# A Fourier filter plus a gated MLP: the first four token tiles transposed in fp32, with another order of instructions

## The chip, the cores and the metric

The kernel runs on one core of a Trainium2 chip. TensorE (PE) multiplies matrices into PSUM; VectorE (DVE) and ScalarE (ACT) work elementwise and read PSUM; GpSimd (POOL) does small work in SBUF; SyncE (SP) issues the DMAs. The metric is the device time of one execution in microseconds (us), the median of several runs.

## The reference

The input x has 2048 tokens of 448 features. The output is a sum of three terms: x itself, a Fourier filter and a gated MLP, the last two on the layer-normalised x.

```python
xn = layernorm(x)                                       # over the 448 features
filter = irfft2(rfft2(xn) * (w_r + 1j * w_i))           # over tokens and features
h = relu(xn @ W_gate) * (xn @ W_up)                     # 448 -> 1792
return x + filter + h @ W_down                          # 1792 -> 448
```

## The kernel before, in words

**Splits.** Every large factor in fp32 is split into a high fp16 part and a low one (the rest), and products are made as high x high + low x high + high x low. So each weight slab costs ACT a scaling to the high half (`whi`, `w_hi`), and DVE a scale-and-subtract to the low half (`wlo`, `w_lo`). Before that ACT squares the slab (`wsq`), GpSimd sums over the partitions (`par`), and DVE makes a power of two from the sum (`wex`, `wsc`). A slab is one of two halves (`g0` gate, `g1` up) of one of 14 blocks (`W0` to `W13`) of the 1792 hidden features; it comes with one 256 KB DMA (`lw`).

**Tokens.** The 2048 tokens lie in 16 tiles `n2` of 128; tile `n2` belongs to chunk q = n2 % 4, and the chunks are worked on in the order 0, 2, 1, 3. A chunk's normalised tokens must stand transposed (features on partitions) as the moving operand: `Tq[q]`, nine rows of [128, 512] fp16. Rows 0 to 2 are the high halves of features 0 to 383, rows 5 to 7 their low halves, and rows 3, 4 and 8 hold the last 64 features, high and low, with a copy of every eighth feature in the other half of the partitions.

**How chunk 0 gets there before.** Its four tiles are loaded (`lx0`, `lx4`, `lx8`, `lx12`), their mean and variance taken on DVE (`bn`, `ag`), and the reciprocal deviation made in two groups A (tiles 0, 4) and B (8, 12) with a square root on ACT (`sq`) and small steps on DVE (`ra` to `rd`, `rm`). Then, for each tile: `xn` (DVE; for tile 4 `an4` on ACT) writes normalised fp32; `hi` (ACT, `ln_hi`) writes its fp16 high half into a tile `tt`; `lo` (DVE, `ln_lo`) the low half; `tpA` and `tpB` (PE, `ln_tp`) transpose three 128x128 fp16 blocks each; `evA` and `evB` (`ln_ev`, a prefix says whether on DVE or ACT) copy them from PSUM into `Tq`. For the last 64 features of all four tiles `tpC` (`ln_tpc`) makes 24 half-width transposes, and three copies (`evC0` to `evC2`, `ln_evc`) bring them to `Tq`. Chunk 2 and the later ones go through fp16 tiles and transposing DMAs (`dm`) instead; the change doesn't touch how they are made.

**Keeping PE busy.** While PE has nothing to do, `keep_warm` issues 512-wide products of a cleared tile into unused PSUM: 16 at the start (`warm`, after GpSimd has cleared that tile) and 4 more a little later (`kw4`).

**The first products.** For block W0 and chunk 0 they are cut up so that they can start early: `hh` (high x high), `lh` (low weight x high tokens), `hl` (high weight x low tokens), each for one of two slabs and one of two 256-column halves (tiles 0 and 4, then 8 and 12): `hh01` is slab 0, half 1. Each has three 256-wide products. `ml` adds the one of rows 3 and 4; then come `hp0` (four products with 64-row weights, shared with W1), and whole slabs `gu1g0`, `gu1g1` and so on. After a block's products ACT and DVE make relu(gate) x up and split it (`re`, `tm`, `gh`, `gl`).

**What sets the order.** The text `OPENING` lists the steps of the opening by these names, and every engine carries out its own in exactly that order (`fixed`). Behind it a planner, `Order.place`, places each instruction by keys and a model of costs (`cost`, `matmul`, `dma`), and its result is the order on each engine. The Fourier filter's work on DVE runs in the background of the MLP, and its matmuls are grouped as 34 "runs" of 64-row shapes (`order.run`), 8 each of four kinds and 2 small ones. A run that is ready interrupts the stream of MLP products only when it has waited longer than its `hold`, when PE is in a 64-row shape already, or when the stream would have to wait. Every instruction appears in the profile under the line of `place` that issues it, L416, so groups are told apart by tile name: `wst` is the loaded slab, `wt` the split weight, `y` fp32 buffers (the tokens of the opening among them), `arena` a region with many small tiles (the `tt` tiles, the identity, the warm tile), `gu`, `dn`, `fx` PSUM banks, `g` and `h` the MLP's results.

Of the kernel before, what the change touches and what calls it, by code (L numbers as in the profile page):

```python
# [34 lines left out]
lx0 lx4 bn0 lx12 bn4 lx8 lw ag0 lid lw ag4 sqA raA rbA rcA warm rdA rmA xn0 bn12 bn8 an4 ag12 hi0 ag8 lo0 hi4 sqB tpA0  # L35
wsqW0g0 lx14 lw tpB0 raB lo4 rbB rcB tpB4 kw4 rdB rmB aevA0 wsqW0g1 lw xn8 tpA4 parW0g0 wexW0g0 lx6 lw vevB4 hi8 vevB0
hi12 wscW0g0 vevA4 whiW0g0 lx10 tpA8 aevA8 tpA12 parW0g1 lo8 tpB8 wsqW1g1 hh00 hl00 wsqW1g0 lw lw lw xn12 vevA12 hh01
lo12 wexW0g1 wloW0g0 parW1 wscW0g1 tpB12 whiW0g1 vevB12 lx2 tpC aevC1 bn6 lwd3 lh01 lh00 wexW1 wscW1 vevB8 hh10 vevC0
whiW1g0 wloW0g1 hl10 wloW1g0 whiW1g1 wloW1g1 hl11 bn10 bn2 bn14 hh11 lwd0 wsqW3g1 ml0 ml1 wsqW2g0 wsqW2g1 lh11 wsqW3g0
parW2 lfd ag2 hl01 ag10 lh10 ag14 ag6 hp0 re0 tm0 lw lwd1 sqC raC wexW2 lw gu1g0 rbC wscW2 rcC rdC xn14 parW3 wexW3  # L40
whiW2g1 wloW2g1 lwd4 gu1g1 hi14 cp14 wscW3 xn2 whiW2g0 lo14 wloW2g0 whiW3g0 hi2 lwd2 whiW3g1 wsqW4g0 xn10 re1 wsqW4g1
parW4 wloW3g0 hi10 cp2 ly0 tm1 gu2g1 gu2g0 cp10 ly4 wdq0 wdq4 wloW3g1 wexW4 gh0 xn6 wdq3 lo10 hp2 gu3g0 hi6 re2 ly12
wscW4 whiW4g0 lo2 whiW4g1 gu3g1 lo6 wdq2 gh1 tm2 dm14 wdq1 gl0 wloW4g0 gu4g0 ly8 dm10 wloW4g1 gl1 cp6 gu4g1 re3 gh2
tm3 wdp wdsc gh3 gl3 aevC2 wdh1 dm2 gl2 wdl1 wdh4 dm6 wdh3 wdl4 hp4 re4 wdl3 tm4 wdh0 wdl0 wdh2 wdl2 gh4 gl4
# [376 lines left out]
def tile_gfnet_reglu(ctx: ExitStack, tc: tile.TileContext, x, xr, wgu, wd, wf, ident, c_fd, c_fm, c_im, c_row, c_id,  # L421
                     out):
    nc = tc.nc
    order = Order()
# [300 lines left out]
    def ln_tpc(q):

        b = (fx(), fx())
        for i in range(3):
            tp["end", i] = b[i // 2].bitcast(F16)[:, 512 * (i % 2):512 * (i % 2) + 512]
        for j in range(4):  # L730
            t = tt[q + 4 * j].rearrange("p a b -> p (a b)")
            c, l = t[:, 384:448], t[:, 1024:1088]
            for i, half in enumerate(((c, t[:, 7:512:8]), (l, c), (l, t[:, 647:1152:8]))):
# [1068 lines left out]
```

## Time and profile before

| | us |
|---|---|
| median of 3 runs | 434.8 (433.99 to 435.23) |
| the profiled execution | 434.42 |
| its span on the core | 432.6 |
| PE / DVE / ACT / POOL busy | 425.2 / 384.0 / 262.7 / 30.1 |
| DMA | 38.63 MB in 37721 packets |

How to read the rows below: a row of a timeline is start, length (both us), engine, line, operation, output <- input by tile name, shape, and count; in brackets the idle time of the engine before it and what ended it. A group's row ends in busy time, mean ns of one, and idle time before. A busy PE row includes the latency of its last product, so the spacing of products is read from several in a row. The length of a PE row is not PE at its peak speed.

### The profile page before, as it was taken

What the parts mean: (1) busy time and instruction counts of PE and PEld (TensorE: products, weight loads), DVE (VectorE), ACT (ScalarE), POOL (GpSimd) and SP (SyncE); (2) the same over time, 40 slices, a digit from 0 to 9 for tenths busy, and PEclk for the clock granted to TensorE, in tenths of its full rate; (3) what the DMA queues carried; (4) which work ended last, traced back from release to release, by engine and by line L of the source; (5) the groups of instructions that cost most, each with busy time, mean ns of one, the idle gap of its engine ahead of it and who ended that gap; (6) DMA issues with size and microseconds to landing.
All of it is one profiled execution on the core that took longest, in us unless ns stands there. A gap on an engine that the chain in (4) does not pass through costs nothing.

```text
span 432.6 us, 8471 instructions
## 1 busy us (share of the span) xinstructions
PE 425.2 (98%) x3222; PEld 202.8 (47%) x3222; DVE 384.0 (89%) x804; ACT 262.7 (61%) x495; POOL 30.1 (7%) x72
## 2 busy tenths in 40 slices
PE   7999999999999999999999999999999999999996
PEld 3644544444444445445444444444554554545554
DVE  6998989999988899999999999999999999993443
ACT  5898466387447938645534634763666765864661
POOL 1140013042001100000000110100000000000000
PEclk9999999999999999999999999999999999999999
DMA  8859319009104703343504300040222121310212
GB/s 258 300 120 258 137 44 233 16 7 218 58 3 131 232 14 113 89 123 84 153 18 104 99 1 0 2 95 8 51 53 45 49 75 24 94 44 2 85 45 86
DMA packets 37721, 38.63 MB, mean 89 GB/s; under 512 B 18928, under 2 KB 33072, under 8 KB 37680
## 3 DMA queue, kind: packets, MB, share of 16 engines
q1 hardware_dynamic: 37680, 38.09, 31.9%
q8 instruction: 25, 0.41, 0.4%
q14 instruction: 16, 0.13, 0.1%
HBM read 23.20 MB, written 3.67 MB: 62 GB/s over the span
## 4 chain that ended last, share of the span: by engine, by line
DVE 47%; PE 34%; ACT 6%; issue 5%; DMA 4%; SPq 3%; DVEq 0%; POOL 0%; ACTq 0%
PE gu L416 23%; DVE y L416 19%; DVE arena L416 13%; PE dn L416 8%; DVE g L416 5%; DVE h L416 4%; PE fx L416 3%; SPq L416 3%; DVE wst L416 2%; ACT arena L416 2%; DVE wt L416 2%; DMA arena<-in_wf 1%; ACT h L416 1%; DMA wst<-in_wgu 1%; ACT y L416 1%
## 5 line engine op out<-in xcount | busy, mean ns | idle before, releaser
L416 PE MATMUL gu<-T,wt 128*128 128x512 f16 (+2 forms) x1250 | 264.4, 376 | 0.0
L416 PEld LDWEIGHTS <-wt 128*128 128x128 f16 (+1 forms) x1250 | 111.4, 97 | 144.0 <-issue 21.6
L416 PE MATMUL dn<-wdt,h 128*128 128x448 f16 x648 | 125.8, 353 | 0.6 <-ACT dn L416 0.5
L416 PEld LDWEIGHTS <-h 128*128 128x128 f16 x684 | 66.0, 98 | 61.8 <-issue 2.6
L416 ACT ACTIVATE h<-g 128x512 f16<-128x512 f32 x56 | 35.1, 628 | 54.5 <-DVE g L416 54.3
L416 DVE TENSOR_TENSOR y<-y 128x464 f32<-128x464 f32 (+2 forms) x82 | 58.8, 745 | 2.3 <-ACT y L416 1.5
L416 DVE TENSOR_TENSOR arena<-arena 128x116 f32<-128x116 f32 (+6 forms) x105 | 52.9, 525 | 4.3 <-ACT arena L416 2.8
L416 ACT ACTIVATE g<-gu 128x512 f32<-128x512 f32 x56 | 32.8, 586 | 34.0 <-PE gu L416 33.9
L416 DVE SCALAR_TENSOR_TENSOR g<-gu,g 128x512 f32<-128x512 f32 x56 | 38.3, 684 | 16.5 <-ACT g L416 13.4
L416 DVE TENSOR_TENSOR h<-g,h 128x512 f16<-128x512 f32 x56 | 38.4, 688 | 4.5 <-ACT h L416 3.8
L416 ACT ACTIVATE xy<-dn,dsc 128x448 f32<-128x448 f32 x44 | 27.5, 625 | 21.0 <-PE dn L416 20.5
L416 DVE TENSOR_TENSOR wst<-wst 128x116 f32<-128x116 f32 (+2 forms) x96 | 30.7, 375 | 0.7
L416 DVE SCALAR_TENSOR_TENSOR y<-y 128x232 f32<-128x232 f32 (+2 forms) x52 | 30.0, 599 | 0.5
L416 ACT ACTIVATE dn<-xy,dinv 128x448 f32<-128x448 f32 x44 | 27.8, 636 | 1.4 <-DMA xy<-in_x 0.3
L416 PEld LDWEIGHTS <-arena 64*128 64x128 f16 (+2 forms) x836 | 17.3, 96 | 14.3 <-issue 6.2
L416 DVE SCALAR_TENSOR_TENSOR wt<-wst,wsc,wt 128x512 f16<-128x512 f32 x28 | 20.2, 745 | 2.3 <-ACT wt L416 2.2
L416 ACT ACTIVATE arena<-arena 128x116 f32<-128x116 f32 (+3 forms) x33 | 15.0, 465 | 10.7 <-DMA arena<-in_wf 7.5
L416 POOL PARTITION_ALL_REDUCE wm<-wm x15 | 8.8, 588 | 175.0 <-DVE y L416 94.3
L416 ACT ACTIVATE wt<-wst,wsc 128x512 f16<-128x512 f32 x28 | 19.0, 711 | 1.8 <-DVE wsc L416 1.8
L416 POOL COPY arena<-arena 128x56 f16<-128x56 f16 (+1 forms) x36 | 15.9, 474 | 59.7 <-ACT arena L416 53.8
L416 ACT ACTIVATE junk<-wst 128x512 bf16<-128x512 f32 x28 | 17.4, 622 | 1.9 <-DMA wst<-in_wgu 1.5
L416 PE MATMUL fx<-arena 64*128 64x64 f16 (+3 forms) x484 | 17.8, 245 | 0.7 <-DVE T L416 0.5
(81 smaller groups left out, 294.2 us busy)
## 6 DMA issues: line engine op xcount, KB each, us to landing
wst<-in_wgu SPq DMA_DIRECT2D x28, 256.0 KB, 4.7
arena<-in_wf SPq DMA_DIRECT2D x16, 232.0 KB, 3.2
arena<-y SPq DMA_DIRECT2D x64, 58.0 KB, 2.0
arena<-wst SPq DMA_DIRECT2D x32, 116.0 KB, 2.3
y<-in_xr SPq DMA_DIRECT2D x16, 224.0 KB, 4.5
xy<-in_x SPq DMA_DIRECT2D x16, 224.0 KB, 4.1
out<-xy SPq DMA_DIRECT2D x15, 224.0 KB, 2.0
wdst<-in_wd SPq DMA_DIRECT2D x14, 224.0 KB, 3.3
```

Of the source, the lines that this page charges most:

```text
L416: fn(*a, **k)
```

## The change

For chunk 0, `xn` now writes fp32 (all four on DVE) straight into the memory of the `tt` tiles, seen as fp32. `tp` transposes three 128x128 fp32 blocks of it against an fp32 identity. `ath` or `vth` (`ln_th`; the order names `ath`, ACT, four times) copies the three blocks from PSUM to fp16, which makes the high half; `tl` (DVE, `ln_tl`) subtracts that from PSUM, which makes the low half. For the last 64 features `tpC` makes 8 fp32 products with the identity. `aend0` (ACT) copies them out as high halves (row 3), `end1` moves half of that to row 4 with a DMA inside SBUF on SP's queue, `end2` (DVE) and `end3` (DVE, late) make the low halves. `hi`, `lo`, `tpA`, `tpB`, `evA`, `evB` and `evC` of chunk 0 are gone. Because the `tt` tiles hold fp32 first, GpSimd clears two regions in each at the start instead of one, and clears one more in each later (`z0` to `z3`).

The warming products become 10 at the start, and `kw1`, `kw1`, `kw5` around `tp0` and `tp4`. The planner gets one waiting time for each of the 34 runs instead of four times 3.0, one margin `SOON` for each engine (0.1 to 0.4) instead of 0.2 for all, a delay of 0.4 for ACT's steps that wait for DVE, and slightly other costs of DVE and of fp32 matmuls. `OPENING` is a new list.

```diff
-NWARM = 16
+NWARM = 10
-HOLDS = 3.0, 3.0, 3.0, 3.0
+HOLDS = (2, 3, 3, 3, 3, 3, 3, 3, 5, 3, 3, 2, 6, 3, 3, 8, 3, 2, 3, 3, 3, 6, 3, 0.5, 10, 5, 0.5, 3, 10, 3, 2, 3, 6, 3)
+SOON = dict(P=0.4, V=0.1, A=0.2, G=0.2, S=0.1)
+LATE = 0.4
+lx0 lx4 bn0 bn4 lx8 ag0 ag4 sqA raA rbA rcA rdA bn8 xn0 lx12 lw warm lid bn12 wsqW0g0 ag8 ag12 sqB kw1 tp0 xn4 rmA raB
+ath0 lw rbB kw1 tp4 rcB lw wsqW0g1 parW0g0 wexW0g0 wscW0g0 lw whiW0g0 rdB tl0 ath4 xn8 xn12 wsqW1g0 wloW0g0 kw5 tp8
+tp12 ath8 tpC parW0g1 wexW0g1 wsqW1g1 wscW0g1 hh00 tl4 tl8 ath12 tl12 parW1 lh00 aend0 wexW1 lx2 wscW1 whiW0g1 whiW1g0
+whiW1g1 wloW0g1 end2 lx6 wloW1g0 wloW1g1 hh01 lwd3 lw lh01 bn6 hl00 lw hl01 hh10 lw hh11 lw lh11 end1 lx14 hl11 lh10
+hl10 ml0 z0 lx10 bn10 ml1 wsqW3g1 bn2 lwd0 hp0 bn14 ag2 wsqW2g0 wsqW2g1 ag10 lwd2 ly4 z1 lw ag14 re0 ag6 wsqW3g0 lwd1
...
-    ISSUE = dict(V=-0.083, A=-0.098, G=-0.06)
-    SOON = 0.2
+    ISSUE = dict(V=-0.079, A=-0.098, G=-0.06)
...
-            return 0.15 + 1.04e-3 * n + 0.06 * ap
+            return 0.155 + 1.042e-3 * n + 0.06 * ap
...
-        return half, quads, 0.42 if x.dtype == F32 else op.n[0] / 2400 + 0.0025
+        return half, quads, (0.42 if rows <= 64 else op.n[0] / 1100) if x.dtype == F32 else op.n[0] / 2400 + 0.0025
...
-            far = 0.04 if op.node.eng == "S" or op.node.fixed else self.SLACK
+            far = dict(S=0.04 if e == "S" or op.node.fixed else self.SLACK)
+            if e == "A" and not op.node.fixed:
+                far["V"] = LATE
...
+    hold = iter(HOLDS).__next__
...
-    id_t = ft([128, 128], F16, "id_t")
+    id_t = ft([128, 128], F32, "id_t")
...
-    for t in tts:
-        G.memset(t[:, 3:9:5, 64:128], 0.0)
+    xts = [t.rearrange("p a b -> p (a b)").bitcast(F32) for t in tts]
+    for t, u in zip(tts, xts):
+        G.memset(u[:, 448:512], 0.0)
+        G.memset(t[:, 8, 64:128], 0.0)
...
+        if n2 % 4 == CHUNKS[0]:
+            xn[n2] = xts[n2 // 4][:, 0:D]
...
+    def ln_zero(i):
+        G.memset(tts[i][:, 3, 64:128], 0.0)
...
+    def ln_tp(n2):
+        j = n2 // 4
+        b = (side[1], *side[0], side[2])[j]
+        tp[n2] = b[:, 0:384].rearrange("p (a b) -> p a b", b=128)
         for a in range(3):
+            P.transpose(tp[n2][:, a, :], xn[n2][:, 128 * a:128 * a + 128], id_t)
...
+    def ln_th(n2, act):
+        js = slice(128 * (n2 // 4), 128 * (n2 // 4) + 128)
+        copy(Tq[n2 % 4][:, 0:3, js], tp[n2], act)
+
+    def ln_tl(n2):
+        T, js = Tq[n2 % 4], slice(128 * (n2 // 4), 128 * (n2 // 4) + 128)
+        V.tensor_tensor(T[:, 5:8, js], tp[n2], T[:, 0:3, js], op=OP.subtract)
...
+        tp["end"] = side[1]
+        for j, x in enumerate(xts):
+            js = slice(128 * j, 128 * j + 128)
+            for h, c in ((0, slice(384, 448)), (1, slice(7, 512, 8))):
+                P.matmul(tp["end"][64 * h:64 * h + 64, js], x[:, c], id_t, start=j == 0, stop=True,
+                         skip_group_check=True)
+
+    def ln_end(q, i, act=False):
+        T, a = Tq[q], tp["end"]
+        if i == 0:
+            copy(T[:, 3, :], a, act)
+        elif i == 1:
+            Q.dma_start(T[64:128, 4, :], T[0:64, 3, :])
+        elif i == 2:
+            V.tensor_tensor(T[0:64, 4, :], a[0:64], T[0:64, 3, :], op=OP.subtract)
+        else:
+            V.tensor_tensor(T[:, 8, :], a, T[:, 3, :], op=OP.subtract)
...
-        with order.run(HOLDS[0]):
+        with order.run(hold()):
```

More of the change, by code (lines that the diff above doesn't have):

```diff
@@ L34 @@
 OPENING = """
[L35 to L44, printed above, removed]
+lx0 lx4 bn0 bn4 lx8 ag0 ag4 sqA raA rbA rcA rdA bn8 xn0 lx12 lw warm lid bn12 wsqW0g0 ag8 ag12 sqB kw1 tp0 xn4 rmA raB
[3 more added lines that the diff above has]
+hl10 ml0 z0 lx10 bn10 ml1 wsqW3g1 bn2 lwd0 hp0 bn14 ag2 wsqW2g0 wsqW2g1 ag10 lwd2 ly4 z1 lw ag14 re0 ag6 wsqW3g0 lwd1
+tm0 sqC gu1g0 parW2 parW3 raC gu1g1 wexW2 re1 rbC wscW2 rcC lw rdC whiW2g1 z2 wexW3 xn14 wscW3 wloW2g1 whiW2g0 wsqW4g0
+whiW3g0 hi14 wsqW4g1 cp14 lwd4 wloW2g0 xn2 hi2 gu2g1 tm1 whiW3g1 lo14 xn10 ly12 cp2 parW4 wloW3g0 gu2g0 wloW3g1 wexW4
+gh0 hi10 hp2 cp10 ly8 z3 xn6 lo10 wdq0 wdq4 hi6 wscW4 ly0 whiW4g0 re2 gu3g1 lo2 gh1 lo6 wdq3 whiW4g1 gu3g0 wdq2
+wloW4g0 end3 tm2 gl0 dm14 wdq1 gl1 dm10 wloW4g1 re3 gu4g0 gh2 cp6 wdp dm2 lfd rmB gu4g1 tm3 dm6 wdsc gh3 gl3 wdh1 hp4
+gl2 wdl1 wdh4 re4 wdh3 wdl4 tm4 wdl3 wdh0 wdl0 wdh2 gh4 wdl2 gl4
 """
@@ L319, in lag @@
             pe = op.node.eng == "P"
-            far = 0.04 if op.node.eng == "S" or op.node.fixed else self.SLACK
-            return max([d.end + (far if d.node.eng == "S" else 0.04) for d in op.deps
-                        if not (pe and d.node.eng == "P")], default=0.0)
+            e = op.node.eng
+            far = dict(S=0.04 if e == "S" or op.node.fixed else self.SLACK)
+            if e == "A" and not op.node.fixed:
+                far["V"] = LATE
+            return max([d.end + far.get(d.node.eng, 0.04) for d in op.deps if not (pe and d.node.eng == "P")],
+                       default=0.0)
         def open_(n):
@@ L351, in pick @@
                 t = [est(n) for n in r]
-                lo = min(t) + self.SOON
+                lo = min(t) + SOON[e]
                 return min(((n, u) for n, u in zip(r, t) if u <= lo), key=lambda v: v[0].key)
@@ L357, in pick @@
                 return None
-            run = min(runs, key=lambda v: (v[1] > free["P"] + self.SOON, v[0].key)) if runs else None
+            run = min(runs, key=lambda v: (v[1] > free["P"] + SOON["P"], v[0].key)) if runs else None
             if head is None:
@@ L365, in pick @@
             now = max(free["P"], max(bank.values()))
-            if self.matmul(head.ops[0])[0][0] == 64 and h[1] <= now + self.SOON:
+            if self.matmul(head.ops[0])[0][0] == 64 and h[1] <= now + SOON["P"]:
                 return h
@@ L719, in copy @@
             V.tensor_copy(o, i)
-    def ln_ev(n2, part, act):
-        q, j = n2 % 4, n2 // 4
-        copy(Tq[q][:, 5 * part:5 * part + 3, 128 * j:128 * (j + 1)], tp[n2, part][:, 0:3], act)
-    def ln_tpc(q):
[L727 to L733, printed above, removed]
-                for h in range(2):
-                    P.transpose(tp["end", i][64 * h:64 * h + 64, 128 * j:128 * j + 128], half[h], id_t)
-    def ln_evc(q, i, act):
-        copy(Tq[q][:, (3, 4, 8)[i], :], tp["end", i], act)
+    def ln_th(n2, act):
[4 more added lines that the diff above has]
+        V.tensor_tensor(T[:, 5:8, js], tp[n2], T[:, 0:3, js], op=OP.subtract)
+    def ln_tpc(q):
+        tp["end"] = side[1]
[12 more added lines that the diff above has]
+            V.tensor_tensor(T[0:64, 4, :], a[0:64], T[0:64, 3, :], op=OP.subtract)
+        else:
+            V.tensor_tensor(T[:, 8, :], a, T[:, 3, :], op=OP.subtract)
     fi, sfx = {}, {}
@@ L826, in f_sdft @@
         sfx[a] = ps
-        with order.run(HOLDS[1]):
+        with order.run(hold()):
             for k in range(2):
@@ L1033, in row_dft @@
         y = state["rowps"] = fx()[:, 0:NG * KC]
-        with order.run(HOLDS[0]):
+        with order.run(hold()):
             for a in range(2):
@@ L1116, in i_sdft @@
         sps[p] = ps
-        with order.run(HOLDS[2]):
+        with order.run(hold()):
             for b in range(2):
@@ L1157, in i_ddft @@
             A.activation(sides[e], xy2[:, a, :, 224 * e:224 * (e + 1)], AF.Copy, scale=fsc[:, 2:3])
-        with order.run(HOLDS[3]):
+        with order.run(hold()):
             for k, n2 in enumerate((a, b)):
@@ L1681, in tile_gfnet_reglu @@
     G.memset(warm, 0.0)
-    wps = dn_bank(), dn_bank()
+    side[1], side[2] = dn_bank(), fx()
+    wps = dn_bank()
     side[0] = gu_bank()
```

47 lines of the change are left out of this document (15 added, 32 removed).

## The prediction

> **What bounds the kernel now.** I read the page's busy line first, then busy time by stretch, then TensorE's (PE's) own timeline of the opening, then the other engines' rows there, and last who waits for whom late in the kernel.
>
> The busy table by stretch gives: us, then busy time of PE, its weight loads (PEld), VectorE (DVE), ScalarE (ACT) and GpSimd (POOL), with counts.
>
> ```profile
> span 432.6 us, 8471 instructions
> PE 425.2 (98%) x3222; PEld 202.8 (47%) x3222; DVE 384.0 (89%) x804; ACT 262.7 (61%) x495; POOL 30.1 (7%) x72
> ...
> 0.00:15.10 15.10, 11.56 (x78) 6.06 (x79) 10.65 (x38) 10.09 (x21) 2.56 (x12) 1.00 0.88 295
> 15.10:43.00 27.90, 27.90 (x192) 13.54 (x192) 25.46 (x67) 25.30 (x56) 6.79 (x16) 1.00 0.73 199
> 43.00:420.00 377.00, 376.40 (x2853) 177.31 (x2852) 343.49 (x692) 225.51 (x416) 20.75 (x44) 1.00 0.28 73
> ```
>
> From 15.1 to 420 us PE is idle for 0.60 us in all (377.00 - 376.40). The kernel is a filled PE stream behind an opening. What can move is the moment at which the stream becomes dense, plus what is lost inside it. Between 15.1 and 43 us DVE (25.46 of 27.90) and ACT (25.30) are close to full too, so an earlier PE needs both of them earlier.
>
> PE's timeline of the opening: start, length, what, count.
>
> ```profile
> 1.89 6.11 PE L416 MATMUL dn<-arena 128*128 128x512 f16 x16 [1.89 <-POOL arena L416]
> 9.45 1.03 PE L416 MATMUL dn<-arena 128*128 128x512 f16 x4
> 12.38 1.15 PE L416 MATMUL gu<-T,wt 128*128 128x256 f16 x9
> 13.50 0.34 PE L416 MATMUL gu<-arena 128*128 128x128 f16 x3
> 13.77 1.38 PE L416 MATMUL fx<-arena 128*64 128x128 f16 x24
> 15.08 1.16 PE L416 MATMUL gu<-T,wt 128*128 128x256 f16 x9
> ```
>
> The 16 products at 1.89 and the four at 9.45 only keep the clock up; the 128x128 and 128x64 rows are transposes. Useful work is the 256-wide pieces: nine between 12.38 and 13.50, at (13.50 - 12.38)/9 = 0.12 us each, then more transposes, and dense pieces from 15.08. Nine pieces at 0.11 are worth 0.98, so PE stands as if it had been dense since **14.1 us**. That is the number the change has to beat.
>
> What the first pieces waited for, from the timeline of all engines and from the landing time of the first weight slab:
>
> ```profile
> 2.61 0.43 SPq L416 DMA_DIRECT2D wst<-in_wgu  x1
> DMA to landing us min/median/max: 4.8/4.8/4.8
> ...
> 3.49 1.19 DVE L416 BATCH_NORM_STATS2 arena<-y 128x6 f32<-128x448 f32 x2 [2.62 <-DMA y<-in_xr]
> 5.46 0.75 DVE L416 SCALAR_TENSOR_TENSOR arena<-arena 128x2 f32<-128x2 f32 x4
> 6.12 0.51 DVE L416 TENSOR_SCALAR y<-y,arena 128x448 f32<-128x448 f32 x1
> 6.24 0.76 ACT L416 ACTIVATE y<-y,arena 128x448 f32<-128x448 f32 x1 [1.01 <-DVE arena L416]
> 6.55 1.15 DVE L416 BATCH_NORM_STATS2 arena<-y 128x6 f32<-128x448 f32 x2
> 6.91 1.40 ACT L416 ACTIVATE arena<-y,arena 128x448 f16<-128x448 f32 x2
> 7.83 0.59 DVE L416 TENSOR_TENSOR arena<-y,arena 128x448 f16<-128x448 f32 x1
> 8.21 0.28 ACT L416 ACTIVATE arena<-arena,eps 128x2 f32<-128x2 f32 x1
> 8.40 0.61 ACT L416 ACTIVATE junk<-wst 128x512 bf16<-128x512 f32 x1
> 9.20 0.40 POOL L416 PARTITION_ALL_REDUCE wm<-wm  x1 [7.37 <-ACT junk L416]
> 11.29 0.71 ACT L416 ACTIVATE wt<-wst,wsc 128x512 f16<-128x512 f32 x1
> ```
>
> The slab is there at 2.61 + 4.8 = 7.4 us, but ACT squares it only at 8.40, behind a normalisation and two high halves (6.24 to 8.3). The scaled weight is ready at 12.0 (11.29 + 0.71), and the first piece follows at 12.38.
>
> **The change part by part.** Chunk 0 is four tiles of tokens. *Removed for it:* on ACT `an4` (0.76) and four `hi` (0.70 each, half of 1.40); on DVE four `lo` (0.59 each); on PE 24 fp16 transposes and the 24 half-width ones of `tpC`; eleven copies out of PSUM, seven on DVE and four on ACT. *Added:* `xn4` on DVE; 12 fp32 transposes and 8 fp32 products (`tpC`); four `ath` and `aend0` on ACT; four `tl`, `end2` and a late `end3` on DVE; one SBUF-to-SBUF DMA (`end1`) on SP's queue; more GpSimd clearing. Prices of what is near:
>
> ```profile
> L416 DVE COPY T<-gu x4: 346/348/350, 10.3 to 15.2; 128x384 f16<-128x384 f16 x4
> L416 ACT ACTIVATE T<-fx x3: 469/490/597, 9.0 to 15.2; 128x384 f16<-128x384 f16 x2, 128x512 f16<-128x512 f16 x1
> L416 DVE SCALAR_TENSOR_TENSOR g<-gu,g 128x512 f32<-128x512 f32 x56 | 38.3, 684 | 16.5 <-ACT g L416 13.4
> ...
> 55.10 1.02 PE L416 MATMUL fx<-arena 64*64 64x464 f32 x8
> 56.05 0.82 PE L416 MATMUL gu<-T,wt 128*128 128x512 f16 x3
> ```
>
> `ath` reads 384 fp32 values where 384 fp16 took 0.49: I take 0.49, less 0.1 where the next instruction starts under its end. `tl` is a two-operand instruction reading PSUM: between 0.35 (the 384-wide copy) and 0.68 (512 wide), near 0.56, because it is of the second kind and a quarter shorter. ACT in sum: 0.76 + 4 x 0.70 + four copies at 0.49 (5.5) out, four `ath` and one wide copy at 0.60 (2.6) in: 2.9 saved. DVE: 4 x 0.59 + 7 x 0.35 (4.8) out, 4 x 0.56 + 0.51 + 2 x 0.68 (4.1) in: 0.7 saved. The later clearings `z0` to `z3` stand on GpSimd, idle for three quarters of that stretch (6.79 of 27.90), ahead of its `cp` copies: nothing, unless the transposing DMAs of chunk 2 become urgent. The identity doubles to 64 KB, behind the first slab on SP's queue: under 0.1 for what follows it.
>
> fp32 on PE: four fp32 products of 464 columns show as eight records, two passes each over four quarters of the array, in 0.95 us (55.10 to 56.05). One pass is thus 0.47 for 464 columns, 0.13 for 128. A fp32 transpose is one pass (0.13) or two (0.26); three make a tile: 0.4 to 0.8. I take 0.4, since a transpose only moves values. `tpC` is 8 plain products of two passes: 2.1 if none overlap, 1.05 if the two column halves run together. The row at 13.77 bears on this: 24 half-width transposes in 1.31 us (13.77 to 15.08), 0.055 each, is one after the other or pairs at half speed. I take 1.05; bounds 0.44 (8 x 0.055) and 2.1. The Trainium skill ("Perfetto Trace Analysis", Transposes) says to use the transpose operation and not a plain matmul for a transpose, as it skips the arithmetic. By that rule `tpC` is the mis-chosen part and the 2.1 end holds, which would leave 0.7 of the gain below; no row here has an fp32 transpose to compare.
>
> *The new opening, engine by engine* (estimates from these rows). DVE starts at 3.49 as before; `rdA` ends at 6.0, as `rmA` has moved back. Then `bn8` 6.2, `xn0` 6.75 to 7.25, `bn12` 7.2, two aggregates to 8.0, `xn4` 8.0 to 8.5, the small steps of B to 9.3 with the exponent of the first slab among them, `tl0` to 9.9, `xn8` to 10.3, `xn12` to 10.8. ACT: the first squares at 7.45, not 8.40; `sqB` 8.05, `ath0` 8.35, squares 8.7, first scaled weight 9.35 to 10.05 (was 12.0), `ath4` to 10.45, squares, `ath8` to 11.45, squares, `ath12` 11.95 to 12.45. PE: `tp8` and `tp12` after `xn8` and `xn12`, done at 11.2; `tpC` to 12.25; `hh00` at **12.3**, with its weight (10.05) and `ath4` there. Nothing that follows is late: `hh01` needs `ath12` (12.45) and runs at 13.0; the second slab's scaled weight comes at 13.6 and `hh10`, 18 pieces after 12.3, at 14.3. So PE is dense from 12.3 against 14.1: **-1.8**.
>
> *What could take it back.* `end1` waits on SP's queue for `aend0` (13.0); behind it stand `lx14`, `lx10`, the `wd` loads and W4. It is needed by `ml0`, 36 pieces of 0.11 after 12.3, at 16.2; 13.05 plus a transfer of 2 to 3 us fits. `bn10` and `bn14`, whose tiles now come after it, are due at 17.3 and 18.4, against 13.5 plus 4.8: they fit by little. Then DVE's weights:
>
> ```profile
> 16.15 2.07 DVE L416 SCALAR_TENSOR_TENSOR wt<-wst,wsc,wt 128x512 f16<-128x512 f32 x3
> 20.39 0.69 DVE L416 SCALAR_TENSOR_TENSOR g<-gu,g 128x512 f32<-128x512 f32 x1 [0.30 <-ACT g L416]
> 26.95 0.74 DVE L416 SCALAR_TENSOR_TENSOR wt<-wst,wsc,wt 128x512 f16<-128x512 f32 x1
> 27.84 0.11 PEld L416 LDWEIGHTS <-wt 64*128 64x128 f16 x4 [0.42 <-DVE wt L416]
> ```
>
> At 27.84 the half-height loads waited for the low half of W3 (26.95 + 0.74): DVE has no slack there. It finishes W1 at 18.2 now and at 16.3 after (`wloW0g1` waits for its high half at 13.6, then `end2` and two more at 0.69): 1.9 earlier. `bn6` moves behind that point (+0.55), and the idle 0.30 before 20.39, with others like it, goes. So W3 comes 1.6 to 1.9 earlier: I carry **-1.7**.
>
> *The rest of the order.* Waiting times, margins and constants of the planner change nothing but the order of instructions from 15 us on. The most that they can win as plain idle time is the 0.60 above. Each half-height group also costs a change of shape:
>
> ```profile
> 18.56 0.12 PEld L416 LDWEIGHTS <-wt 64*128 64x128 f16 x4 [0.21 <-issue]
> 19.10 0.11 PEld L416 LDWEIGHTS <-wt 128*128 128x128 f16 x2 [0.42 <-issue]
> PE dn L416 <- ACT dn L416: 0.5, 1, 0.5
> ```
>
> Four half-height products that two and two share PE need 2 x 0.22 = 0.43 us and took 0.54 (18.56 to 19.10), so a change of shape costs about 0.1 on the way out and as much again in. Spectral runs that join such a group save 0.2 each; five of 34 make 1.0. In the other direction, one misplaced seed cost 0.5 (the last row). Bounds -1.5 and +0.8; I take **-0.3**, nearer to nothing, as PE is already full.
>
> **Sum.** 434.42 (profiled execution, 432.6 of span) - 1.7 - 0.3 = 432.4; it lies 0.4 under the median 434.8, so against the median **432.8**.
>
> **The rivals.** *R1, fp32 costs double on PE.* With two passes a transpose and no overlap, `tp8` ends at 11.2, `tp12` at 12.0, `tpC` at 14.1: PE is dense from 14.1, exactly as now. Only the order's share is left: 434.8 - 0.3 = **434.5**. For it: the two passes of the fp32 row, and the 0.055 of `tpC` now. Against: halves go to different columns.
>
> *R2, the order gains too.* Some five joined runs and the idle half: 434.8 - 1.7 - 1.4 = **431.7**. For it: the losses are visible; against: each is small, and joining delays a run that DVE waits for.
>
> *R3, the clock stays low, and the kernel is slower.* The weight loads of the warming products:
>
> ```profile
> 6.13 0.15 PEld L416 LDWEIGHTS <-arena 128*128 128x128 f16 x1 [0.28 <-issue]
> 6.56 0.15 PEld L416 LDWEIGHTS <-arena 128*128 128x128 f16 x1 [0.28 <-issue]
> 6.97 0.53 PEld L416 LDWEIGHTS <-arena 128*128 128x128 f16 x3 [0.26 <-issue]
> 0.74 1.09 POOL L416 MEMSET arena<- 128x128 f16 x5 [0.29 <-POOLq L1790]
> ```
>
> Products come every 0.43 us up to 6.56 and every 0.21 after 6.97: the speed doubles 5 us after the first one (the page's clock column says 1.00 throughout and doesn't show it). Four more clearings, about 0.14 us each, put the first product at 2.3 to 2.4; ten and one at 0.43 end at 7.1, 4.7 us later, just short. If the doubling is missed and the transposes don't bring it, `kw5` takes 2.1 us (to 11.1), `tp8` and `tp12` end at 12.7, `tpC` at 14.8, and pieces run at half speed for 5 us, which loses 2.5: dense as if from 17.3, +3.2, so **437.7**. It decides at `kw5`: at 0.21 apart, R3 is out. Against it: between 8.0 and 12.4 now, PE does four such products and transposes only, and the pieces at 12.38 run at full speed. The Trainium skill ("TensorE: Matmul & The Clock Gate", Part 4) says that the fast clock doesn't engage for transposes, which don't count as busy. That speaks for R3; the four fast microseconds above show only that it isn't lost at once.
>
> **How the numbers follow.** About 0.3%, 1.3 us, is what a measurement of this kernel can tell from no change: faster is under 433.5, slower over 436.1. Forecast 0.50 (431.9 to 433.4: the opening between 1.3 and 2.0, the order between 0 and 0.9); R1 in whole or half, 0.24 (433.5 to 434.8); R2 0.13; R3 0.08; an order that loses half a microsecond and more, 0.05 (to 435.2). Faster is 0.50 + 0.13 = 0.63, same 0.24 + 0.05 = 0.29, slower 0.08. The range goes from R2's better end, 430.9, to 435.2 and leaves out R3 and the tails.
>
> **What would show it.** Right: squares of the first slab near 7.45; `hh00` near 12.3; PE with no hole from 13.0 on; low half of W3 near 25.2; idle PE from 43 us on under 0.6. Wrong: `tpC` longer than 1.5 (R1), products of `kw5` 0.43 apart (R3), PE waiting for a DMA or for `end2` before `ml0`, or a hole before W2's weights.

## The result, and the profile after

The changed kernel takes 432.43 us (median of 7 executions, 431.17 to 433.6), the one before 434.45 (7 executions beside them, 433.99 to 435.23). The ratio is 0.995 with a 95% interval of 0.9929 to 0.997: 2.0 us less, more than the 0.3% that the prediction named as the limit of what can be told. The profiled execution is the best of the seven: 431.17 (429.4 of span), 3.25 under the profiled one of before. What a profile shows is therefore over a microsecond better than what the median shows; a part below is about that.

First the changed kernel's page (span, busy time by engine, the chain that ended last):

```profile
span 429.4 us, 8425 instructions
PE 422.9 (98%) x3199; PEld 202.1 (47%) x3199; DVE 375.7 (87%) x800; ACT 259.8 (61%) x491; POOL 31.1 (7%) x80
PE 97%; DMA 1%; DVE 0%; SPq 0%; ACT 0%; issue 0%
```

The chain is now PE and hardly anything else (before: DVE 47%, PE 34%). Then PE in the opening, from its timeline (start, length, operation, tile shape, count, idle time ahead of it and who ended that):

```profile
7.53 0.73 PE L420 MATMUL dn<-arena 128*128 128x128 f32 x4 [1.00 <-DVE arena L420]
8.10 0.53 PE L420 MATMUL gu<-arena 128*128 128x128 f32 x3
8.46 1.24 PE L420 MATMUL dn<-arena 128*128 128x512 f16 x5
9.98 0.55 PE L420 MATMUL gu<-arena 128*128 128x128 f32 x3 [0.27 <-DVE arena L420]
10.40 0.55 PE L420 MATMUL fx<-arena 128*128 128x128 f32 x3
10.88 1.25 PE L420 MATMUL dn<-arena 128*64 128x128 f32 x16
12.06 6.26 PE L420 MATMUL gu<-T,wt 128*128 128x256 f16 x47
```

The gate/up pieces start at 12.06 and no hole follows, against "as if from 14.1" before: 2.04 earlier. A tile of three fp32 transposes takes 0.42 (9.98 to 10.40) to 0.48 (10.40 to 10.88), with one record for each transpose, so they are single passes of 0.14 to 0.16. `tpC` shows 16 records for 8 products, two passes each, and takes 1.18 (10.88 to 12.06).

The other engines in the same stretch, and where W3's low half ends (all engines' timeline):

```profile
7.21 0.63 ACT L420 ACTIVATE junk<-wst 128x512 bf16<-128x512 f32 x1 [2.08 <-DMA wst<-in_wgu]
8.08 0.49 ACT L420 ACTIVATE T<-dn 128x384 f16<-128x384 f32 x1
8.95 0.55 DVE L420 TENSOR_TENSOR T<-dn,T 128x384 f16<-128x384 f32 x1
9.08 0.71 ACT L420 ACTIVATE wt<-wst,wsc 128x512 f16<-128x512 f32 x1
24.12 1.44 DVE L420 SCALAR_TENSOR_TENSOR wt<-wst,wsc,wt 128x512 f16<-128x512 f32 x2
25.80 0.12 PEld L420 LDWEIGHTS <-wt 64*128 64x128 f16 x4 [0.42 <-DVE wt L420]
```

`ath` takes 0.49 and `tl` 0.55, as the prediction took them (0.49, 0.56). The first slab's squares start at 7.21 (7.45 forecast), its scaled weight ends at 9.79 (10.05). W3's low half ends at 25.56 and its loads come at 25.80; before they came at 27.84. The profile puts the 0.42 of idle time ahead of them down to that weight, but the same 0.42 stands before a change of shape that waited for nothing (at 19.10, in the prediction), and PE's own timeline has no hole here.

Last, three spectral runs that both kernels have at the same place of the stream, picked from PE's timelines in pairs, before (L416) and after (L420), and PE over the middle stretch of the changed kernel (window, length, busy time and count of PE, PEld, DVE, ACT, POOL, granted clock, DMA share, GB/s):

```profile
48.56 0.80 PE L416 MATMUL fx<-arena,T 64*128 64x58 f16 x46
46.38 0.80 PE L420 MATMUL fx<-arena,T 64*128 64x58 f16 x46
185.50 0.36 PE L416 MATMUL fx<-arena,row_t 128*128 128x232 f16 x2
182.90 0.36 PE L420 MATMUL fx<-arena,row_t 128*128 128x232 f16 x2
331.99 0.78 PE L416 MATMUL fx<-idc_t,arena 64*128 64x56 f16 x48
328.77 0.78 PE L420 MATMUL fx<-idc_t,arena 64*128 64x56 f16 x48
```

```profile
43.00:420.00 377.00, 377.00 (x2858) 177.79 (x2855) 335.79 (x692) 225.32 (x415) 21.04 (x44) 1.00 0.27 72
```

The lead is 2.18 at 47 us (48.56 to 46.38), 2.60 at 183 us (185.50 to 182.90) and 3.22 at 329 us (331.99 to 328.77); the spans end 3.2 apart (432.6 and 429.4). PE's idle time in the middle is nil, against 0.60 before, and yet the lead grows by 1.04 there. It is still 2.2 at 127 us and 2.6 at 261, so it grows at two places, both at the seed of a down-projection output, that is ACT's instruction that fills its PSUM bank ahead of the products. The first stands before only in the row of the weight loads, since the length of a PE row covers it:

```profile
172.70 0.64 ACT L416 ACTIVATE dn<-xy,dinv 128x448 f32<-128x448 f32 x1
173.39 2.55 PEld L416 LDWEIGHTS <-h 128*128 128x128 f16 x14 [0.39 <-issue]
```

The changed kernel has no such gap in its loads there. The second is the hole that PE's own row shows; the all-engine timeline of before tells why:

```profile
311.19 1.06 ACT L416 ACTIVATE arena<-arena 128x1024 f16<-128x1024 f32 x1 [1.12 <-DVE arena L416]
312.15 0.62 ACT L416 ACTIVATE xy<-dn,dsc 128x448 f32<-128x448 f32 x1
312.80 0.64 ACT L416 ACTIVATE dn<-xy,dinv 128x448 f32<-128x448 f32 x1
...
313.49 3.00 PE L416 MATMUL dn<-wdt,h 128*128 128x448 f16 x15 [0.46 <-ACT dn L416]
```

ACT works in the order of its list. A spectral step (the 1024-wide one) waits 1.12 for DVE, and the two instructions behind it, post and seed of a down-projection output, are what PE then waits for. The weight loads are idle for 0.72 there. The new constant `LATE` makes the planner count 0.4 for ACT's waits on DVE, where it counted 0.04.

### The profile page after: what moved, and what is told of

It reads as the page before. It is cut to its first block, busy times and chain, and to the rows that moved or that the text cites. A ratio compares the mean times of both kernels' runs of the same rounds, so it can differ in the third digit from the quotient of the medians.

```text
span 429.4 us, 8425 instructions
## 1 busy us (share of the span) xinstructions
PE 422.9 (98%) x3199; PEld 202.1 (47%) x3199; DVE 375.7 (87%) x800; ACT 259.8 (61%) x491; POOL 31.1 (7%) x80
## 4 chain that ended last, share of the span: by engine, by line
PE 97%; DMA 1%; DVE 0%; SPq 0%; ACT 0%; issue 0%
PE gu L420 62%; PE dn L420 29%; PE fx L420 6%; DMA wst<-in_wgu 1%; SPq L420 0%; DVE arena L420 0%; ACT junk L420 0%; DVE xy L420 0%; ACT arena L420 0%; DVE wsc L420 0%; DVE eg L420 0%; DVE T L420 0%
## 5 line engine op out<-in xcount | busy, mean ns | idle before, releaser
L420 PE MATMUL gu<-T,wt 128*128 128x512 f16 (+2 forms) x1250 | 264.0, 377 | 0.0
L420 PEld LDWEIGHTS <-wt 128*128 128x128 f16 (+1 forms) x1250 | 111.5, 98 | 144.0 <-issue 19.4
L420 PE MATMUL dn<-wdt,h 128*128 128x448 f16 x648 | 125.8, 353 | 0.0
L420 PEld LDWEIGHTS <-h 128*128 128x128 f16 x684 | 66.1, 98 | 61.0 <-issue 1.5
L420 ACT ACTIVATE g<-gu 128x512 f32<-128x512 f32 x56 | 33.1, 591 | 57.3 <-PE gu L420 57.3
L420 DVE TENSOR_TENSOR y<-y 128x464 f32<-128x464 f32 (+2 forms) x82 | 58.9, 742 | 1.2 <-DMA row<-y 0.6
L420 DVE SCALAR_TENSOR_TENSOR g<-gu,g 128x512 f32<-128x512 f32 x56 | 38.4, 686 | 23.7 <-ACT g L420 19.3
L420 ACT ACTIVATE h<-g 128x512 f16<-128x512 f32 x56 | 35.0, 624 | 36.6 <-DVE g L420 36.4
L420 DVE TENSOR_TENSOR arena<-arena 128x116 f32<-128x116 f32 (+6 forms) x105 | 52.9, 526 | 3.9 <-ACT arena L420 2.8
L420 ACT ACTIVATE xy<-dn,dsc 128x448 f32<-128x448 f32 x44 | 27.7, 630 | 33.2 <-PE dn L420 33.1
L420 DVE TENSOR_TENSOR h<-g,h 128x512 f16<-128x512 f32 x56 | 38.2, 685 | 2.7 <-ACT h L420 2.5
L420 DVE TENSOR_TENSOR wst<-wst 128x116 f32<-128x116 f32 (+2 forms) x96 | 30.7, 372 | 0.2
L420 DVE SCALAR_TENSOR_TENSOR y<-y 128x232 f32<-128x232 f32 (+2 forms) x52 | 30.3, 598 | 0.2
L420 ACT ACTIVATE dn<-xy,dinv 128x448 f32<-128x448 f32 x44 | 27.7, 636 | 2.3 <-DMA xy<-in_x 1.2
L420 DVE SCALAR_TENSOR_TENSOR wt<-wst,wsc,wt 128x512 f16<-128x512 f32 x28 | 20.4, 748 | 5.0 <-ACT wt L420 5.0
L420 POOL COPY arena<-arena 128x56 f16<-128x56 f16 (+1 forms) x36 | 16.8, 505 | 56.7 <-ACT arena L420 53.6
L420 POOL PARTITION_ALL_REDUCE wm<-wm x15 | 8.3, 552 | 170.6 <-ACT junk L420 149.6
L420 ACT ACTIVATE junk<-wst 128x512 bf16<-128x512 f32 x28 | 17.4, 623 | 3.0 <-DMA wst<-in_wgu 2.8
L420 ACT ACTIVATE wt<-wst,wsc 128x512 f16<-128x512 f32 x28 | 19.0, 710 | 0.2 <-DVE wsc L420 0.2
L420 PEld LDWEIGHTS <-arena 64*128 64x128 f16 (+1 forms) x785 | 14.2, 95 | 10.1 <-issue 5.7
L420 ACT ACTIVATE arena<-arena 128x116 f32<-128x116 f32 (+3 forms) x33 | 14.8, 464 | 6.1 <-DMA arena<-in_wf 3.1
L420 DVE TENSOR_TENSOR y<-y,arena 128x928 f32<-128x928 f32 x16 | 17.9, 1121 | 0.3
```

Source lines behind the costliest of these rows:

```text
L420: fn(*a, **k)
```

## The experiments

Every ratio is against the kernel before on the same chip. Times are medians; batches share their runs of before (434.08, 433.87, 434.04 and 434.23).

**order_only** keeps the opening of before and takes the new planner numbers alone; **opening_only** is the other half. The numbers include the planner's cost of a transposing DMA (1.37 to 1.5). The edit of the second, and in the first the reverse beside the whole old opening:

```diff
-HOLDS = (2, 3, 3, 3, 3, 3, 3, 3, 5, 3, 3, 2, 6, 3, 3, 8, 3, 2, 3, 3, 3, 6, 3, 0.5, 10, 5, 0.5, 3, 10, 3, 2, 3, 6, 3)
-SOON = dict(P=0.4, V=0.1, A=0.2, G=0.2, S=0.1)
-LATE = 0.4
+HOLDS = (3.0,) * 34
+SOON = dict(P=0.2, V=0.2, A=0.2, G=0.2, S=0.2)
+LATE = 0.04
-    ISSUE = dict(V=-0.079, A=-0.098, G=-0.06)
+    ISSUE = dict(V=-0.083, A=-0.098, G=-0.06)
-            return 0.155 + 1.042e-3 * n + 0.06 * ap
+            return 0.15 + 1.04e-3 * n + 0.06 * ap
-            return 1.5, 1.78, 1.55
+            return 1.37, 1.78, 1.55
```

> The opening of before, with the planner's new waiting times, margins and constants. Theory A (two thirds of the gain is the opening, the rest is two holes in the later stream, 0.3 and 0.6 us, that the new order doesn't have): about 0.9 us under the kernel before, 433.5, and PE idle between 43 and 420 us under 0.1 instead of 0.6. Rival B (the new order carries the gain, the opening's lead is eaten up by DVE): 2 us under, 432.4. Rival C (the holes close by chance of the opening, the constants do nothing): no change, 434.4.

> The new opening with the old waiting times, margins and constants of the planner. Theory A: first dense pieces at 12.06 as in the changed kernel, 2.2 us ahead of before at 40 us and kept to the end, so 432.2 in a run with a full clock; holes of half a microsecond may be back. Rival B: the lead shrinks after 43 us, 433.7. Rival C: the holes are gone too, 431.3 with a full clock.

order_only: 433.33 (433.26 to 433.43), ratio 0.9983 (0.9974 to 0.9992): 0.75 less, as Theory A had it, and PE has no idle time from 43 to 420 us. opening_only: 435.67 (434.8 to 436.42), ratio 1.0033 (1.002 to 1.0045): 1.6 *more* than before, which no theory had. Two things are in its trace. The waits of PE from 43 to 420 us (total, times, longest), with PE's busy time there:

```profile
PE dn L420 <- ACT dn L420: 1.8, 2, 1.3
PE fx L420 <- ACT y L420: 0.3, 1, 0.3
PE gu L420 <- DMA T<-arena: 0.3, 1, 0.3
PE gu L420 <- DVE g L420: 0.2, 1, 0.2
```

```profile
43.00:420.00 377.00, 374.41 (x2841) 176.19 (x2840) 341.55 (x691) 223.79 (x415) 20.98 (x44) 1.00 0.28 74
```

2.6 us of holes, most of them at down-projection seeds; the longest ends at 315.5 us, behind the same 1024-wide step of ACT as above. And PE's clock came late (its timeline in the opening):

```profile
8.71 0.84 PE L420 MATMUL gu<-arena 128*128 128x128 f32 x3
9.35 2.11 PE L420 MATMUL dn<-arena 128*128 128x512 f16 x5
11.29 0.49 PE L420 MATMUL gu<-arena 128*128 128x128 f32 x3
11.62 0.49 PE L420 MATMUL fx<-arena 128*128 128x128 f32 x3
12.04 1.25 PE L420 MATMUL dn<-arena 128*64 128x128 f32 x16
13.22 7.12 PE L420 MATMUL gu<-T,wt 128*128 128x256 f16 x51
```

The five warming products take 2.11 us here, 0.43 apart: R3, in small. The pieces start at 13.22, not 12.06. The granted clock of this execution reads 1.000 all the same.

**no_kw** and **more_warm** ask what the warming is worth: none between the transposes, or three products more at the start and one more in two places.

```diff
 no_kw (the names kw1, kw1 and kw5 leave the opening's list)
-... ag8 ag12 sqB kw1 tp0 xn4 rmA raB
-ath0 lw rbB kw1 tp4 rcB ... wloW0g0 kw5 tp8
+... ag8 ag12 sqB tp0 xn4 rmA raB
+ath0 lw rbB tp4 rcB ... wloW0g0 tp8
 more_warm
-NWARM = 10
+NWARM = 13
-ath0 lw rbB kw1 tp4 rcB ... wloW0g0 kw5 tp8
+ath0 lw rbB kw2 tp4 rcB ... wloW0g0 kw6 tp8
```

> The changed kernel without the seven warming products between the transposes (kw1, kw1, kw5). The order on all other engines stays the same. Theory D (the scatter of the changed kernel from 431.2 to 433.6, with granted clocks of 1.000, 0.999 and 0.996, is clock lost in the opening): more executions at 0.996 and below, median 433.5 or more. Rival E (the scatter comes from elsewhere, the products are idle work): median 432.4 and the same mix of clocks.

> The changed kernel with 13 warming products at the start, not 10, and kw2 and kw6 in place of the second kw1 and of kw5: the hole of 1.2 us before the first fp32 transpose is filled. All else is in the same order. Theory D: hardly any execution under clock 1.000, times between 431.1 and 431.8, median near 431.4. Rival E: median 432.4 and the same scatter; a cold start that delays the first transpose by up to 0.4 us would show as 432.8.

no_kw: 433.77 (433.11 to 434.05), ratio 0.9992 (0.9984 to 1.0001). PE's timeline, and one microsecond of the table by stretch, with the granted clock as the third number from the end:

```profile
8.09 0.55 PE L420 MATMUL gu<-arena 128*128 128x128 f32 x3
9.99 0.68 PE L420 MATMUL gu<-arena 128*128 128x128 f32 x3 [1.35 <-DVE arena L420]
10.46 0.85 PE L420 MATMUL fx<-arena 128*128 128x128 f32 x3
11.24 1.99 PE L420 MATMUL dn<-arena 128*64 128x128 f32 x16
13.16 7.14 PE L420 MATMUL gu<-T,wt 128*128 128x256 f16 x50
```

```profile
12.00:13.00 1.00, 1.00 (x12) 0.82 (x8) 0.94 (x4) 0.18 (x1) 0.54 (x3) 0.50 0.93 346
```

The first transposes run at full speed, those from 10.46 on at half: the clock falls about 4 us after the last wide product, and `tpC` costs 1.92. The granted clock is 0.50 from 10.4 to about 13.6, which over the whole span makes the 0.996 of this execution (half of 3.2 us is 0.4% of 431.8). The other ten executions show 0.992 to 1.000, and the three at 0.999 or 1.000 are no faster (433.51 to 433.9), so this average alone doesn't sort the times. Two of the changed kernel's own seven executions, 433.6 and 433.56, have the same 0.996; the other five have 0.999 or 1.000. That the clock fell in those two as in no_kw is likely from the number and from the time, but neither was profiled.

more_warm: 431.66 (431.12 to 431.95), ratio 0.9942 (0.9929 to 0.9954), 2.4 less than before and, among runs of the same batch, 2.1 less than no_kw. Its interval overlaps the changed kernel's, so the medians alone don't part the two; but of the 20 executions with this warming in more_warm, mw_late0, mw_hold3 and mw_xn8 (below) none is over 432.47. With older planner numbers it doesn't hold: mw_old_late, warmed in the same way, reaches 432.98.

**mw_late0, mw_hold3, mw_old_late** and, later, **mw_old** take the planner's numbers apart on more_warm's opening, where the clock doesn't disturb.

```diff
 mw_late0: only LATE goes back
-LATE = 0.4
+LATE = 0.04
 mw_hold3: only the list goes back
+HOLDS = (3.0,) * 34
 mw_old_late: everything of opening_only's edit but LATE goes back
 mw_old: everything of it goes back
```

> As more_warm (2.4 us under the kernel before), but the planner's delay for ACT's steps that wait for DVE goes from 0.4 back to 0.04; PE's order stays the same, ACT's and DVE's change. Theory F (the delay keeps ACT from standing in front of a late DVE result while a seed for PE waits behind it): holes at dn<-ACT dn come back, 0.5 to 2 us in all, so 0.5 to 1.9 under before. Rival G (the waiting times of the runs close the holes): as more_warm, 2.4 under.

> As more_warm, with 3.0 for all 34 runs in place of the list. Theory F: within 0.5 us of more_warm, so 1.9 to 2.4 under before. Rival G: half of the gain or more goes, 1.2 under before or less, with holes in PE after 43 us.

> As more_warm, but with all the old planner constants except the delay of 0.4 (waiting times 3.0, margins 0.2, old costs). Theory F: the delay alone closes the holes at dn<-ACT dn, 1.8 us of them in opening_only, so 2 us under before and PE idle from 43 us on under 0.5. Rival G: the holes stay, 1 us over before as opening_only was 1.6 over.

> As mw_old_late, with the delay back at 0.04: all the old planner constants, under the new opening with more warming. It closes the square with opening_only, mw_old_late and mw_late0. Theory F2 (the delay for ACT and the other new constants each suffice to close the holes, only the full old set opens them): 0.5 over the kernel before, holes of 2.5 us and more in PE, the longest at dn<-ACT dn. Rival L (opening_only was slow because its clock was low until 10.8 us): as mw_old_late, 1.5 under before.

mw_late0: 431.7, ratio 0.995 (0.9938 to 0.9962). mw_hold3: 431.55, 0.9945 (0.9933 to 0.9957). mw_old_late: 432.38, 0.9962 (0.9948 to 0.9977). mw_old: 434.12, 0.9999 (0.9989 to 1.0008). The theory that `LATE` is what closes the holes fell with mw_late0, which lost nothing and has none. The list of 34 waiting times alone is worth nothing that can be measured (mw_hold3). But mw_old, with all the old numbers, gains nothing at all, although its pieces start at 12.27; its waits from 43 to 420 us, and PE's busy time there (the profiled execution is the longest of its 12):

```profile
PE dn L420 <- ACT dn L420: 2.0, 2, 1.0
PE gu L420 <- DMA T<-arena: 0.6, 1, 0.6
```

```profile
43.00:420.00 377.00, 374.40 (x2841) 176.01 (x2840) 341.64 (x691) 224.27 (x415) 20.66 (x44) 1.00 0.28 73
```

The two seeds are those of before and of opening_only (near 174 and 314 us). Giving it `LATE` alone (mw_old_late) closes every hole and brings 1.6; giving it the rest without `LATE` (mw_late0) closes them as well and brings 2.1, both by the ratios. So either is enough, and of the sets tried only the full old one opens them. Between mw_old and opening_only lie 1.5 us with the same old numbers, and the warming is all that differs; 0.95 of it shows in the start of the pieces (12.27 and 13.22).

**mw_xn8, mw_sqb and order_sq** move steps of the opening, to ask what sets its end.

```diff
 mw_xn8 (DVE: the third normalisation ahead of the first low half)
-... rdB tl0 ath4 xn8 xn12 ...
+... rdB xn8 tl0 ath4 xn12 ...
 mw_sqb (ACT: B's deviations ahead of the first squares; the tiles' steps ahead of the first scaled weight)
-... warm lid bn12 wsqW0g0 ag8 ag12 sqB kw1 tp0 ...
+... warm lid bn12 ag8 ag12 sqB wsqW0g0 kw1 tp0 ...
-... wsqW0g1 parW0g0 wexW0g0 wscW0g0 lw whiW0g0 rdB tl0 ath4 xn8 xn12 wsqW1g0 wloW0g0 kw6 tp8
-tp12 ath8 tpC ... wsqW1g1 wscW0g1 hh00 tl4 tl8 ath12 tl12 ... wscW1 whiW0g1 whiW1g0
+... rdB xn8 wsqW0g1 parW0g0 lw tl0 xn12 ath4 kw3 tp8 ath8 wexW0g0 wscW0g0 whiW0g0 wsqW1g0 wloW0g0
+tp12 ath12 tpC ... wscW0g1 hh00 tl4 tl8 whiW0g1 wsqW1g1 tl12 ... wscW1 whiW1g0
 order_sq (order_only, with the first slab ahead of the tiles on ACT)
-... rmA xn0 bn12 bn8 an4 ag12 hi0 ...
+... rmA xn0 bn12 bn8 an4 wsqW0g0 ag12 hi0 ...
-... rdB rmB aevA0 wsqW0g1 ... parW0g0 wexW0g0 ... hi12 wscW0g0 vevA4 whiW0g0 ...
+... rdB parW0g0 wexW0g0 wscW0g0 rmB aevA0 whiW0g0 wsqW0g1 ... hi12 vevA4 ...
```

> As more_warm, with xn8 ahead of tl0 on DVE. In the changed kernel PE waits at 9.98 us for xn8 (the last hole before the dense stream). Theory H (the dense stream starts when xn8 is there): tp8 at 9.5, the stream 0.4 earlier at 20 us, and the same at the end if DVE's weights keep up, 2.8 under before. Rival I (DVE's weights W1 and W3 set the pace right behind, as the waits for wt at 16.5 and 25.8 us say): the lead is gone by 26 us, 2.4 under before.

> As more_warm, with the square root of group B ahead of the first slab's squares on ACT, rdB, xn8, tl0 and xn12 ahead of the first slab's exponent on DVE, and kw3 in place of kw6; a reorder of the opening alone. Theory N (in the six profiles of this opening the dense stream follows the landing of the first slab, 7.13 us to 11.97 and 7.95 to 12.91, because sqB and with it tp8 stand behind the squares): dense stream near 11.7 whatever the landing, median 431.0 and less scatter. Rival I (DVE's weights set the pace right behind): same median as more_warm, 431.6, less scatter.

> The old opening under the new planner constants (order_only), with the first slab's squares on ACT ahead of the high halves, and its exponent and scaling ahead of tiles 8 and 12: the order alone of the new opening, without the fp32 transposes. Theory A (ACT has too much work before the first dense products; only taking the high halves away frees it): the scaled weight comes 1 us earlier, the tokens later, dense stream not before 15.0; 0.3 to 0.9 under before, no better than order_only. Rival M (the early squares are the gain): 1.5 to 2.2 under before.

mw_xn8: 431.39 (431.23 to 432.47), ratio 0.995 (0.9938 to 0.9962): no gain over more_warm that can be told. mw_sqb: 433.06 (432.74 to 433.64), 0.9979 (0.997 to 0.9989): 1.6 more than more_warm by the ratios, although the pieces start earlier (11.91 against 12.29). Both its expectations, 431.0 and 431.6, missed. PE's timeline:

```profile
11.91 2.93 PE L420 MATMUL gu<-T,wt 128*128 128x256 f16 x24
15.27 5.00 PE L420 MATMUL gu<-T,wt 128*128 128x256 f16 x29 [0.42 <-DVE wt L420]
```

PE waits 1.7 us in all for weights in its first 43 us. The stream has two suppliers, the tiles and the weights, and what is taken from the second is lost right behind the start. order_sq says the same from the other side: 435.67 (435.32 to 436.19), 1.0038 (1.0026 to 1.005), 2.4 more than order_only by the ratios, where both theories had a gain. The first squares now hold up ACT's `hi` steps, and PE waits 2.8 us for these. This new order of the old steps doesn't give the early start; that none does, so that ACT and DVE had to be relieved of steps first, fits, but one order doesn't show it.

**mw_tpc2** doubles the disputed cost: `tpC` is computed twice, with the same result.

```diff
-        for j, x in enumerate(xts):
+        for j, x in 2 * list(enumerate(xts)):
```

> As more_warm, with the eight fp32 products of tpC issued twice into the same bank (the second set starts it anew; the result is the same), all else in the same order: 1.2 us more PE work ahead of the first dense product. Theory P (PE's own work in the opening is on the path, as rival R1 of the prediction assumed): dense stream 1.2 later and 1.2 lost at the end, 1.2 under the kernel before. Theory I (DVE's and ACT's weights pace the stream right behind): the wait for wt at W1 and W3 takes up part of it, 0.5 to 0.9 lost, 1.5 to 1.9 under.

mw_tpc2: 433.76 (432.98 to 434.78), ratio 0.9989 (0.9979 to 0.9998), some 2.0 over more_warm. PE's timeline:

```profile
11.68 2.23 PE L420 MATMUL dn<-arena 128*64 128x128 f32 x32
13.84 6.47 PE L420 MATMUL gu<-T,wt 128*128 128x256 f16 x48
```

Sixteen products take 2.16, so eight more cost 0.98. The time grows by more, 2.0: neither expectation holds (1.2 or 1.5 to 1.9 under before; measured 0.5), and the idea that part of the doubling would be absorbed was wrong. `aend0` waits 0.99 for `tpC` in ACT's queue with high halves of weights behind it, and in the profiled execution PE then waits 0.9 for weights, against 0.2 in more_warm. How much of that is the doubling stays open, since the first weight slab also landed late in this execution (squares at 8.01), as the next table shows for others.

**What the median has that the best profile has not.** Across the runs with this opening and the new order or its like, one number read from the profiles, when ACT's first squares start (they wait for the first weight slab, whose DMA was issued at 2.6 in each), goes with the time of the same execution. These are six kernels with one profile each, not six executions of one:

| kernel | first squares | pieces from | time of that execution |
|---|---|---|---|
| mw_late0 | 7.13 | 11.97 | 431.08 |
| the changed kernel | 7.21 | 12.06 | 431.17 |
| more_warm | 7.45 | 12.29 | 431.71 |
| mw_old_late | 7.69 | 12.54 | 432.05 |
| mw_hold3 | 7.71 | 12.56 | 431.92 |
| mw_xn8 | 7.95 | 12.91 | 432.47 |

ACT's timeline of mw_xn8 shows the path:

```profile
7.95 0.63 ACT L420 ACTIVATE junk<-wst 128x512 bf16<-128x512 f32 x1 [2.81 <-DMA wst<-in_wgu]
...
8.57 0.28 ACT L420 ACTIVATE arena<-arena,eps 128x2 f32<-128x2 f32 x1
```

`sqB`, the deviations of tiles 8 and 12, stands behind squares that wait for a DMA: 0.8 us of landing move both suppliers; the pieces move by 0.94 and the time from 431.1 to 432.5, of which the last 0.4 is not traced. mw_sqb takes `sqB` out of that shadow. Its executions spread by 0.9 (9 of them), which is less than in mw_xn8 (1.2 of 5) but not than in more_warm (0.8 of 5), so a smaller scatter is not shown. For the changed kernel itself, landing and clock can't be parted: only one execution has a profile, and its seven also fall into groups by granted clock (431.2 to 431.4 at 1.000, 432.4 at 0.999, 433.6 at 0.996).

## Why the prediction was right, and where it was not

- **The total** (432.8 forecast, 432.43 measured) and the sign hold. The range of 430.9 to 435.2 holds every execution of the changed kernel. That the number is so close is partly luck. The sum was made for a profiled execution, 432.4, and that one came at 431.17, as both terms were larger than taken; the median lies 1.26 above it where the sum had 0.4, and late landings and lost clock are the likely causes.
- **The opening** (carried as -1.7): right in mechanism, slightly small. The pieces start 0.24 before the forecast 12.3, and the squares started 0.24 before the forecast 7.45: one landing, no step of the working. more_warm bears that out: its squares start at 7.45 and its pieces at 12.29. W3's low half, which the forecast had 1.6 to 1.9 earlier, ends 2.13 earlier (25.56, was 27.69). The 25.2 in the prediction's list of signs doesn't follow from its own working, which gives 25.8 to 26.1. That W3 has no slack is right: in more_warm, PE itself waits 0.2 for it.
- **fp32 on PE**: the value taken for `tpC` (1.05) was near the 1.18 measured; transposes are single passes (0.4 per tile taken, 0.42 to 0.48 measured). **R1 fell** on both. The Trainium skill ("Perfetto Trace Analysis", Transposes) spoke against plain products here. The trace agrees so far as each such product costs two passes where a transpose costs one. That the 2.1 end follows, as the prediction read it, was wrong: 16 passes of 0.14 to 0.16 would take over 2.2 one after the other, and take 1.18, so the column halves overlap. Whether the same eight as transposes would be shorter still, no run here shows.
- **The order** (-0.3): the step "the rest of the order" was mis-sized, and its form failed. In the profile it is -1.04. The bound of 0.60 on plain idle time was read from PE's rows, which hide the gap at 173.39; the weight loads show it. More important, it was added to the opening as a term of its own. It isn't one: the order alone is worth 0.75 (order_only), the new opening under the old numbers nothing, even with the warming secured (mw_old, 434.12 against 434.04), and both together 2.0 to 2.4. A lead of two microseconds at 12 us survives only if everything that PE needs later is in time for it, and the old planner, given the new opening, places two seeds behind waits of ACT and one gate/up group behind a DMA. That -1.7 and -0.3 add up to the measured 2.0 is thus no proof of the two terms.
- **R2** (the order gains as well) is half right, by another mechanism: the holes vanished, and joining is not what did it. Counted in the weight-load timelines, there are 47 stretches of 64-row loads before and 46 after.
- **R3** (the clock) was weighed as all or nothing, and occurs in small: in opening_only's profile through a late start, in no_kw's through a fall, and probably in 2 of the changed kernel's 7 executions (0.996), 1.1 to 1.2 over the median. The step that failed is "the speed doubles 5 us after the first one", a rule made from one profile. In mw_tpc2 the doubling came about 3 us after the first product, in more_warm more than 5.1 us after (products still 0.43 apart at 7.07), in opening_only about 9 us after; in the changed kernel's profile the products are still 0.43 apart at 5.79 and the transposes run at full speed from 7.5 on. The first product came at 1.97, against 1.89 before, not at 2.3 to 2.4, as the eight clearings are shorter ones (151 ns each, against 204 for the four before). The Trainium skill ("TensorE: Matmul & The Clock Gate", Part 4) says that transposes don't count as busy; no_kw, where the clock fell although six transposes had run, agrees with it, but PE was also idle for most of those 4 us, and no run here parts the two.
- **"Nothing" for `end1`, GpSimd's clearings and the larger identity** stood: PE waits for none of them in the changed kernel. The prediction's exception were the transposing DMAs of chunk 2: the profile names one of them as what the weight loads at 35.09 waited for, without a hole on PE.

Left open: which of `SOON`, the duration constants and the DMA constant closes the holes when `LATE` is absent, and whether the planner would meet such holes again after the next small edit. No run joined `LATE` with each of them singly.

The best version by its ratio is more_warm: 431.66 against 434.08 before, with none of its 5 executions above 431.95. mw_hold3, which has its opening and plain waiting times, mw_late0 and mw_xn8 can't be told from it.

## What to carry to other kernels

An earlier start is worth only what the whole chain behind it lets through: after each change of an opening, look at the bottleneck's idle time over the rest of the span (PE's in the row of its weight loads too), and at in-order queues in which a step that waits for another engine stands ahead of one that the bottleneck needs. Two edits that each look like a term of a sum may only work together; run each alone and both, before one of them is thrown away. And compare medians with the spread of what a profile fixes by chance (when the first load lands, when the clock opens), as the profile shows one draw of it.

## What the runs showed of the hardware

- An fp32 transpose of 128x128 is one pass of 0.14 to 0.16 us; an fp32 plain product with 64 output columns shows two passes, and 8 of them take 1.18 us, 16 take 2.16. At 0.14 a pass, that is about half of what they would take one by one, so the two column halves work side by side.
- PE's speed doubled at different times after the first product under the same instructions (by 7.5 us in the changed kernel's profile, near 11 in opening_only's, first product at 2.0 in both). In no_kw it was lost again about 4 us after the last wide product, when only transposes ran in between. The profile's clock shows the loss (0.50 in no_kw) but not the slow start, for which it reads 1.00; the spacing of the weight loads shows both. Here it is in opening_only (PEld's timeline), still 0.43 at 10.63:

```profile
10.20 0.15 PEld L420 LDWEIGHTS <-arena 128*128 128x128 f16 x1 [0.28 <-issue]
10.63 0.15 PEld L420 LDWEIGHTS <-arena 128*128 128x128 f16 x1 [0.28 <-issue]
```

- The same first weight load, issued at 2.6 us in each of six kernels' profiles, let ACT start between 7.13 and 7.95 us, a stretch of 0.8; the time of the profiled execution went with it, from 431.08 to 432.47.
